# A spectral filter with a gated feed-forward part on one core: a rebuilt prologue, another layout of an intermediate, and stage C moved in the schedule

## The chip, the cores and the metric

The kernel runs on 1 core of one Trainium2 chip. The metric is device time in microseconds (us). "Before" is the kernel before the change, "after" the changed kernel.

## The reference

```python
# x: (8, 3008, 256) float32, filters: (1505, 256)
X = np.fft.rfft(x, axis=1)
y = np.fft.irfft(X * (filt_r + 1j * filt_i), n=3008, axis=1)
t = y.reshape(24064, 256)
gate = np.maximum(t @ w_gate, 0)          # (24064, 1536)
out = (gate * (t @ w_val)) @ w_out        # (24064, 256)
```

## The kernel before

The length 3008 is factored as 94 x 32, so the Fourier part becomes matmuls, done per batch in three stages. Stage A makes the 94-point transform in fp32 and writes it to DRAM (`Abuf`), from where it is read back with other partitions into `at`. Stage B makes the 32-point transform, the product with the filters, and the inverse 32-point transform, and writes the result to DRAM (`Dbuf`), from where it is read into `dC`. Stage C makes the inverse 94-point transform straight into `yT`, the input of the feed-forward part.

The feed-forward part is 47 blocks of 512 tokens, each of 12 steps (`ft`), 564 steps in all. The stages of the next batch are threaded into these steps by hand. Batch 0 is done ahead of them, in a prologue.

```python
def items_a(b):                           # 16 items, one matmul of 512 columns each
    def one(c, j, st):
        psA = ps.tile([128, 512], FP32, tag=fft_tag(), name="psA")
        nc.tensor.matmul(psA[0:NROW], WA[:, :NROW], XF[...][:, o:o + 512], start=True, stop=True)
        nc.scalar.copy(st["asb"][:, j * 512:(j + 1) * 512], psA[0:NROW])
        if j == 3:                        # every fourth item: 384 KB to DRAM
            nc.sync.dma_start(_ap(Abuf[b], ...), st["asb"])
# ...
def load_at(b, c):                        # a quarter of at, after the quarter of Abuf is written
    nc.sync.dma_start(ats[b][32 * c:32 * c + 32], _ap(Abuf[b], ...))
# ... items_b(b): 12 x fwd(g) (psX, then tt and uu), with inv() (psD, then dsb, then Dbuf) two items later
def load_d(b):
    for z in range(NZ):
        dC = sb.tile([NROW, 4, D], BF16, tag="dC", bufs=12)
        nc.sync.dma_start(dC, _ap(Dbuf[b], z * 4 * D, [[N2 * D, NROW], [1, 4 * D]]))
# ... the prologue, from stage B of batch 0 on
for i, f in enumerate(items_b(0, 1)):     # one filler matmul (warm) in each item
    f()
    if i == 4:
        load_vg(2)                        # last third of the value and gate weights
warm(28)                                  # 28 fillers during D's way through DRAM
load_d(0)
hold_gpsimd(dCs[0, 0][0:32, 0, 0:8])      # GpSimd reads dC, so its later loads wait for it
load_o()
load_x(1, nc.gpsimd)
for h in range(2):
    item_c(0, h)
# ... the schedule
LAST = 9
for b in range(1, B):
    end = (b * S // W - 1) * NFT + LAST - 5
    if b == 1:
        s0, sb0 = 13, 33
        every = [sb0 + i + i // 2 for i in range(14)]
    else:
        s0 = end - 54                                     # A starts
        every = [(s0 + 24 | 1) + 2 * i for i in range(14)]  # B starts 25 steps later
    for i, f in enumerate(items_a(b)):
        at_step(s0 + i, f)
    for c in range(4):
        at_step(s0 + 6 + 4 * c, lambda b=b, c=c: load_at(b, c))
    if b + 1 < B:
        at_step(s0 + 17, lambda b=b: load_x(b + 1, nc.gpsimd))
    for i, f in zip(every, items_b(b)):
        at_step(i, f)
    at_step(every[-1] + 1, lambda b=b: load_d(b))
# ... in each step: gate and value matmuls, output matmuls of the last block, the side items, and
if ft in (LAST - 2, LAST + 1) and k + 1 < NB:
    item_c(k + 1, 0 if ft < LAST else 1)
```

In the names of the profile, `psA` is a product of stage A, `psX` and `psD` are the first and the second product of stage B, `psY` is that of stage C, and `psG`, `psV` and `psO` belong to the feed-forward part; `XF` is the input x on the chip. A filler is a matmul whose result (`psJ`) nobody uses; it only keeps TensorE busy.

Of the kernel before, what the change touches and what calls it, by code (L numbers as in the profile page):

```python
# [25 lines left out]


N1, N2 = 94, 32
NROW = 96
NG = 24  # L30
# [9 lines left out]
def _tables():  # L40
    n1 = np.arange(N1)
    n2 = np.arange(N2)
    p = np.arange(16)
    wa = np.zeros((128, NROW + 2))
    for a in range(2):
        wa[np.arange(128) // 16 % 2 == a, NROW + a] = 1.0
    part = 4 * (n1 % 32) + n1 // 32
# [4 lines left out]
    i2t = np.zeros((128, NG, 64))  # L52
    i2u = np.zeros((128, NG, 64))
    for hg in range(48):
        g, a = divmod(hg, 2)
        rows = slice(a * 64, a * 64 + 64)
        f = np.zeros((64, 64))
        t = np.zeros((64, 64))
        u = np.zeros((64, 64))
        k1 = 2 * hg + 2 if hg < 23 else 0 if hg == 23 else 2 * (hg - 24) + 1  # L60
        th = 2 * np.pi * ((n1 * k1) % N1) / N1
        wa[part, 2 * hg] = np.cos(th)
        if k1 not in (0, 47):
            wa[part, 2 * hg + 1] = -np.sin(th)
            m1[2 * hg] = 2.0 * np.cos(th) / S
            m1[2 * hg + 1] = -2.0 * np.sin(th) / S
            k = np.stack([k1 + N1 * p, S - (N1 * (p + 1) - k1)], 1).reshape(32)
            conj = np.tile([1.0, -1.0], 16)
            th = 2 * np.pi * (np.outer(n2, k) % S) / S
            c, s = np.cos(th), np.sin(th)  # L70
            f[:] = np.block([[c, -s], [s, c]])
            ct, st = c.T, s.T
            t[:] = np.block([[ct, st], [-st, ct]])
            u[:] = np.block([[-st, ct], [-ct, -st]]) * np.concatenate([conj, conj])[:, None]
        else:
            m1[2 * hg] = np.cos(th) / S
            th = 2 * np.pi * (np.outer(n2, k1 + N1 * p) % S) / S
            c, s = np.cos(th), np.sin(th)
            f[0:32, 0:32:2] = c
            f[0:32, 32::2] = -s  # L80
            t[0:32:2, 0:32] = 2.0 * c.T
            t[32::2, 0:32] = -2.0 * s.T
            u[0:32:2, 0:32] = -2.0 * s.T
            u[32::2, 0:32] = -2.0 * c.T
            if k1 == 0:
                sign = np.where(n2 % 2 == 0, 1.0, -1.0)
                f[0:32, 32] = sign
                t[0, 0:32] = 1.0
                t[32, 0:32] = sign
                u[0] = 0.0  # L90
                u[32] = 0.0
        f2[lo + 16 * a, g] = f
        i2t[rows, g], i2u[rows, g] = t, u
    tab = np.stack([f2, i2t, i2u], 1).reshape(128, 3, 2, NG // 2, 64).transpose(0, 2, 1, 3, 4)
# [4 lines left out]
def kernel(  # L99
# [31 lines left out]

    Abuf = [dram.tile([NROW * N2, D], BF16, name=f"Abuf{b}") for b in range(B)]
    Dbuf = [dram.tile([NROW * N2, D], BF16, name=f"Dbuf{b}") for b in range(B)]

    WA = consts.tile([128, NROW + 2], FP32)
    XF = [consts.tile([128, NX2 * D], FP32, name=f"XF{c}") for c in range(N2 // NX2)]
# [31 lines left out]
    def place_tables(half):  # L168
        gs = slice(half * H, half * H + H)
        for a in range(2):  # L170
            nc.vector.tensor_scalar(F2[:, gs, a * 64:a * 64 + 64], tabs[:, half, 0],
                                    WA[:, NROW + a:NROW + a + 1], None, op0=ALU.mult)
        for i, t in ((1, I2t), (2, I2u)):
            for a in range(2):
                r = slice(a * 64, a * 64 + 64)
                nc.vector.tensor_copy(t[r, gs, a * 64:a * 64 + 64], tabs[r, half, i])

    def load_filters(half):

        first = 2 - half  # L180
        for fi, (src, dst) in enumerate(FILT):
            for a in range(2):
                r = a * 64
                k1, n = first + 2 * a, H - a
                gs = slice(H * half, H * half + n)
                nc.gpsimd.dma_start(dst[r:r + 31:2, gs, :],
                                    _ap(src, k1 * D, [[N1 * D, 16], [4 * D, n], [1, D]]))
                nc.gpsimd.dma_start(dst[r + 1:r + 32:2, gs, :],
                                    _ap(src, (N1 - k1) * D, [[N1 * D, 16], [-4 * D, n], [1, D]]))
        if half == 0:  # L190
            for fi, (src, dst) in enumerate(FILT):
                nc.gpsimd.dma_start(dst[64:95:2, H - 1::H, :],
                                    _ap(src, 0, [[N1 * D, 16], [47 * D, 2], [1, D]]))
                nyq[fi] = pro.tile([1, D], BF16, tag="nyq", bufs=2, name="nyq")
                nc.gpsimd.dma_start(nyq[fi], _ap(src, (S // 2) * D, [[D, 1], [1, D]]))

    nyq = {}

    def place_filters(half):

        gs = slice(H * half, H * half + H)
        for fi, (src, dst) in enumerate(FILT):
            for a in range(2):
                r = a * 64
                if half == 0:
                    nc.vector.tensor_copy(dst[r + 32:r + 64, gs, :], dst[r:r + 32, gs, :])
                else:
                    nc.sync.dma_start(dst[r + 32:r + 64, gs, :], dst[r:r + 32, gs, :])
            if half == 0:
                nc.vector.tensor_copy(dst[96:97, H - 1, :], nyq[fi])  # L210

    def load_vg(c):
        w = DFF // 3
        for (w_hbm, w_sb) in ((moe_w_val, WvT), (moe_w_gate, WgT)):
            nc.gpsimd.dma_start(w_sb[:, :, c * w:(c + 1) * w],
                                _ap(w_hbm, c * w, [[DFF, 128], [128 * DFF, 2], [1, w]]))

# [6 lines left out]
    def hold_gpsimd(tile_):  # L224

        scr = pro.tile([32, 8], tile_.dtype, tag="scr", bufs=1)
        nc.gpsimd.tensor_copy(scr, tile_)
# [26 lines left out]

    GC = 6
    ats = {}

# [5 lines left out]

    def items_b(b, junk=0):

# [4 lines left out]
        def fwd(g):  # L270
# [6 lines left out]
            nc.vector.tensor_tensor(tt, psX, Ftr[:, g:g + 2, :], op=ALU.mult)  # L277
            if b == 0 and g % 4 == 2:
                xs = pro.tile([128, 2, D], FP32, tag="xs", bufs=2)
# [6 lines left out]
        def inv():  # L286
# [10 lines left out]
            if g + 2 in cuts:  # L297
                nc.sync.dma_start(_ap(Dbuf[b], st["g"] * 128 * D,
                                      [[D, 128], [128 * D, o + 2], [1, D]]), st["dsb"][:, :o + 2, :])

        for g in range(0, NG, 2):
            def both(g=g):
                fwd(g)
                if junk:
                    warm(junk)
                if len(held) > 2:
                    inv()
            yield both
# [4 lines left out]

    def load_d(b):
        for z in range(NZ):
            dC = sb.tile([NROW, 4, D], BF16, tag="dC", bufs=12)
            nc.sync.dma_start(dC, _ap(Dbuf[b], z * 4 * D, [[N2 * D, NROW], [1, 4 * D]]))
            dCs[b, z] = dC
# [83 lines left out]
    load_x(0, nc.sync, 2 * q)  # L402
    for t in (I2t, I2u):
        nc.vector.memset(t, 0.0)
    for (src, dst) in FILT:
        for g in (H - 1, NG - 1):
            nc.vector.memset(dst[64:128, g, :], 0.0)
    load_filters(0)
    load_filters(1)

# [8 lines left out]
    load_at(0, 3)  # L419
    warm(26)  # L420
    place_tables(0)
    place_filters(0)
    place_tables(1)
    place_filters(1)
    hold_gpsimd(ats[0][96:128, NG - 1, 0:8])
    load_vg(0)
    load_vg(1)

    for i, f in enumerate(items_b(0, 1)):
        f()  # L430
        if i == 4:
            load_vg(2)
    warm(28)
    load_d(0)
    hold_gpsimd(dCs[0, 0][0:32, 0, 0:8])
    load_o()
    load_x(1, nc.gpsimd)
    for h in range(2):
        item_c(0, h)
    prologue.close()  # L440
    fs = ctx.enter_context(tc.tile_pool(name="fs", bufs=2))
# [6 lines left out]

    LAST = 9
    for b in range(1, B):  # L450
        end = (b * S // W - 1) * NFT + LAST - 5
        if b == 1:
            s0, sb0 = 13, 33
            every = [sb0 + i + i // 2 for i in range(14)]
        else:
            s0 = end - 54
            every = [(s0 + 24 | 1) + 2 * i for i in range(14)]
        for i, f in enumerate(items_a(b)):
            at_step(s0 + i, f)
        for c in range(4):  # L460
            at_step(s0 + 6 + 4 * c, lambda b=b, c=c: load_at(b, c))
        if b + 1 < B:
            at_step(s0 + 17, lambda b=b: load_x(b + 1, nc.gpsimd))
        for i, f in zip(every, items_b(b)):
            at_step(i, f)
        at_step(every[-1] + 1, lambda b=b: load_d(b))
    prev = None
    for k in range(NB):
        prods = []
        for ft in range(NFT):  # L470
# [3 lines left out]
            for f in side.get(k * NFT + ft, ()):  # L474
                f()
            if ft in (LAST - 2, LAST + 1) and k + 1 < NB:
                item_c(k + 1, 0 if ft < LAST else 1)
        prev = (k, prods)
# [30 lines left out]
```

## Time and profile before

| | before |
|---|---|
| median of the first three runs | 1013.98 us |
| span of the profiled run | 1011.3 us |
| TensorE busy | 956.4 us |
| first feed-forward matmul | 62.2 us |

The page's first part gives busy time, its share of the span and the number of instructions; its fourth part follows the chain of work that ended last, back from the end, and sums it by engine. Two lines of before:

```profile
PE 956.4 (95%) x5934; PEld 567.5 (56%) x6044; DVE 545.6 (54%) x825; ACT 522.2 (52%) x938; POOL 51.5 (5%) x85
...
PE 88%; DMA 5%; ACT 2%; DVE 2%; issue 1%; POOL 1%; SPq 0%; ACTq 0%; POOLq 0%
```

TensorE (PE) is the limit nearly everywhere, so what matters is when it stands still. The view of waits lists for TensorE: which group waited, for whom, us in total, how often, the longest. From it, for before:

```profile
PE psY L338 <- ACT dsb L296: 9.4, 14, 0.7
PE psX L274 <- DMA Fti<-Fti: 7.4, 1, 7.4
PE psX L274 <- DMA at<-Abuf_72: 7.1, 1, 7.1
PE psY L338 <- DMA dC<-Dbuf_80: 5.5, 1, 5.5
PE psD L294 <- POOL uu L281: 3.2, 4, 1.0
```

The reader should see one long list item made of many small waits (`psY` for `dsb`: 9.4 us in 14 waits, wherever a C item falls into a step of B), and three single waits of 5 to 7 us, each for a transfer. Buffers are numbered through the whole program: `Abuf_71` is batch 0 and `Abuf_72` batch 1 in both kernels, but `Dbuf_80` is batch 1 before and batch 0 after.

The table of windows gives, for a stretch in us from the start, its length, the busy time of each engine with its instructions, the granted TensorE clock, the busy share of the DMA engines, and GB/s. Around the wait for `at` of batch 1, before:

```profile
116.00:120.00 4.00, 0.75 (x5) 0.39 (x4) 0.73 (x2) 0.56 (x1) 0.00 (x0) 1.00 0.65 256
120.00:124.00 4.00, 0.11 (x1) 0.11 (x2) 0.00 (x0) 0.00 (x0) 0.00 (x0) 0.60 0.44 115
124.00:128.00 4.00, 4.00 (x20) 2.26 (x20) 2.45 (x4) 0.58 (x1) 0.00 (x0) 0.55 0.00 0
128.00:132.00 4.00, 3.88 (x26) 2.34 (x24) 3.51 (x7) 2.35 (x5) 0.00 (x0) 1.00 0.20 57
```

After some 7 us of idling TensorE runs at about half clock (0.55) for 4 us more, so this wait costs more than its length.

### The profile page before, as it was taken

To read this page: it belongs to the slowest core of one execution; us is meant where nothing else is said; L and a number is where in the kernel's file an instruction comes from. 1 tells how busy PE (TensorE), PEld (TensorE's weight loads), DVE (VectorE), ACT (ScalarE), POOL (GpSimd) and SP (SyncE) were. 2 spreads that over 40 slices of the span, in tenths; PEclk is the share of its full clock that TensorE was granted. 3 is DMA by queue.
4 is the path that set the end of the run, shared out by engine and by line. 5 is a ranking of instruction groups with operands and counts; after the bars stand their busy time and mean duration, and the time that the engine had idled before them with its cause. 6 is when DMAs were issued, how large, how long until landed. Compare 5 with 4: busy or idle time off the path is not lost.

```text
span 1011.3 us, 16206 instructions
## 1 busy us (share of the span) xinstructions
PE 956.4 (95%) x5934; PEld 567.5 (56%) x6044; DVE 545.6 (54%) x825; ACT 522.2 (52%) x938; POOL 51.5 (5%) x85
## 2 busy tenths in 40 slices
PE   8699797999999999999999999999999999999996
PEld 3345364546665556655666456654666556666664
DVE  4443384436754367534865357543675437755551
ACT  3255354555555555555555555555555555555552
POOL 5420000000000100000000000000000000000000
PEclk9899898999999999999999999999999999999998
DMA  9994524154232622436123452415423241231111
GB/s 257 201 266 132 160 53 115 31 175 121 76 110 53 214 74 53 115 92 206 47 71 93 131 172 53 119 38 160 133 77 109 53 115 48 57 112 37 32 32 43
DMA packets 98544, 107.08 MB, mean 106 GB/s; under 512 B 7940, under 2 KB 87236, under 8 KB 96836
## 3 DMA queue, kind: packets, MB, share of 16 engines
q1 hardware_dynamic: 89488, 78.98, 29.0%
q0 software_dynamic: 8576, 25.86, 9.2%
q8 instruction: 47, 0.77, 0.3%
q10 hardware_dynamic: 400, 1.20, 0.3%
q14 instruction: 33, 0.27, 0.1%
HBM read 59.31 MB, written 49.81 MB: 108 GB/s over the span
## 4 chain that ended last, share of the span: by engine, by line
PE 88%; DMA 5%; ACT 2%; DVE 2%; issue 1%; POOL 1%; SPq 0%; ACTq 0%; POOLq 0%
PE psG L354 24%; PE psO L372 23%; PE psV L354 22%; PE psA L243 10%; PE psY L338 2%; PE psX L274 2%; PE psD L294 2%; PE psD L293 2%; DVE prod L359 1%; ACT vsb L357 1%; DMA XF_89<-in_x_dram 1%; ACT dsb L296 1%; DMA Abuf_72<-asb 1%; PE psJ L391 1%; DMA Abuf_71<-asb 1%
## 5 line engine op out<-in xcount | busy, mean ns | idle before, releaser
L359 DVE SCALAR_TENSOR_TENSOR prod<-psG,vsb 128x512 bf16<-128x512 f32 x564 | 389.8, 691 | 397.5 <-ACT vsb L357 381.0
L357 ACT CAST vsb<-psV 128x512 bf16<-128x512 f32 x564 | 331.1, 587 | 223.1 <-PE psV L354 140.6
L372 PE MATMUL psO<-WoT,prod 128*128 128x256 bf16 x2256 | 339.1, 274 | 3.2 <-ACT osb L378 2.5
L354 PE MATMUL psG<-yT,WgT 128*128 128x512 bf16 x1107 | 332.2, 380 | 4.2 <-issue 0.2
L354 PE MATMUL psV<-yT,WvT 128*128 128x512 bf16 x1041 | 318.3, 380 | 1.8 <-ACT yT L343 0.4
L372 PEld LDWEIGHTS <-prod 128*128 128x128 bf16 x2256 | 221.7, 98 | 147.9 <-issue 4.5
L354 PEld LDWEIGHTS <-WgT 128*128 128x128 bf16 x1128 | 110.3, 98 | 135.2 <-issue 2.8
L354 PEld LDWEIGHTS <-WvT 128*128 128x128 bf16 x1128 | 104.5, 98 | 66.4 <-issue 55.5
L246 ACT CAST asb<-psA 96x512 bf16<-96x512 f32 x128 | 74.3, 581 | 120.2 <-PE psA L243 117.0
L296 ACT CAST dsb<-psD 128x512 bf16<-128x512 f32 x96 | 55.9, 586 | 57.0 <-PE psD L294 55.6
L277 DVE TENSOR_TENSOR tt<-psX,Ftr 128x512 bf16<-128x512 f32 x96 | 65.1, 681 | 21.2 <-PE psX L274 21.2
L378 ACT COPY osb<-psO 128x512 f32<-128x512 f32 (+1 forms) x96 | 55.3, 576 | 33.1 <-PE psO L372 27.1
L243 PE MATMUL psA<-XF_89,WA 128*96 128x512 f32 x128 | 65.0, 592 | 1.5 <-DMA XF_89<-in_x_dram 1.5
L243 PE MATMUL psA<-XF_88,WA 128*96 128x512 f32 x128 | 65.1, 592 | 0.4 <-DMA XF_88<-in_x_dram 0.4
L283 DVE TENSOR_TENSOR uu<-psX,Fti 128x512 bf16<-128x512 f32 x90 | 61.2, 680 | 0.0
L274 PE MATMUL psX<-at,F_91 128*128 128x256 bf16 x192 | 37.8, 280 | 15.6 <-DMA Fti<-Fti 7.4
L338 PEld LDWEIGHTS <-dC 96*128 96x128 bf16 x604 | 34.8, 98 | 31.7 <-issue 23.8
L338 PE MATMUL psY<-M_90,dC 96*128 96x94 bf16 (+18 forms) x604 | 37.8, 199 | 14.9 <-ACT dsb L296 9.4
L294 PE MATMUL psD<-uu,I2u 128*128 128x256 bf16 x192 | 47.2, 273 | 3.2 <-POOL uu L281 3.2
L293 PE MATMUL psD<-tt,I2t 128*128 128x256 bf16 x192 | 47.5, 273 | 0.0
L343 ACT CAST yT<-psY 128x512 bf16<-128x512 f32 x47 | 27.5, 585 | 30.8 <-PE psY L338 30.7
L345 DVE CAST yT<-psY 128x512 bf16<-128x512 f32 x47 | 32.1, 684 | 17.3 <-PE psY L338 17.2
(47 smaller groups left out, 202.0 us busy)
## 6 DMA issues: line engine op xcount, KB each, us to landing
XF_88<-in_x_dram POOLq DMA_DIRECT2D x20, 512.0 KB, 7.6
XF_89<-in_x_dram POOLq DMA_DIRECT2D x20, 512.0 KB, 7.7
out_dram<-osb SPq DMA_DIRECT2D x72, 94.0 KB
XF_88<-in_x_dram SPq DMA_DIRECT2D x6, 256.0 KB
XF_89<-in_x_dram SPq DMA_DIRECT2D x3, 512.0 KB
Abuf_71<-asb SPq DMA_DIRECT2D x4, 384.0 KB
at<-Abuf_71 SPq DMA_DIRECT2D x4, 384.0 KB
dC<-Dbuf_79 SPq DMA_DIRECT2D x8, 192.0 KB
```

The lines of the kernel that those rows point to most:

```text
L243: nc.tensor.matmul(psA[0:NROW], WA[:, :NROW], XF[c * NC2 // NX2][:, o:o + 512], start=True, stop=True)
L246: nc.scalar.copy(dst, psA[0:NROW])
L277: nc.vector.tensor_tensor(tt, psX, Ftr[:, g:g + 2, :], op=ALU.mult)
L283: nc.vector.tensor_tensor(uu, psX, Fti[:, g:g + 2, :], op=ALU.mult)
L293: nc.tensor.matmul(psD[:, i], I2t[:, g + i, :], tt[:, i], start=True, stop=False)
L294: nc.tensor.matmul(psD[:, i], I2u[:, g + i, :], uu[:, i], start=False, stop=True)
L296: nc.scalar.copy(st["dsb"][:, o:o + 2, :], psD)
L338: nc.tensor.matmul(psY[:, o:o + w], dCs[b, n2 // 4][:, n2 % 4, h * 128:(h + 1) * 128], M1[:, n1:n1 + w], start=True, stop=True)
L354: nc.tensor.matmul(pt[:, :W], w[:, h, ft * 128:(ft + 1) * 128], yt[:, h, :], start=(h == 0), stop=(h == 1))
L357: nc.scalar.copy(vsb, psV[:, :W])
L359: nc.vector.scalar_tensor_tensor(prod, in0=psG[:, :W], scalar=0.0, in1=vsb, op0=ALU.max, op1=ALU.mult)
L372: nc.tensor.matmul(psO[:, t % 2], prods[ft][:, t * 128:(t + 1) * 128], WoT[:, ft, :], start=(ft == 0), stop=(ft == NFT - 1))
```

## The change

The intent is to start the feed-forward part with more work done: the first stage A items of batch 1 run amid and after stage B of batch 0 in place of filler matmuls. For this x of batch 1 is loaded early, the filters are loaded in longer runs, the tables are placed with a mask, and D is written in runs of 3 KB and read in runs of 512 B. C moves to steps 8 and 10, which B (odd steps) never uses. The diff, cut to its core:

```diff
-            m1[2 * hg] = 2.0 * np.cos(th) / S
-            m1[2 * hg + 1] = -2.0 * np.sin(th) / S
+            m1[48 * a + g] = 2.0 * np.cos(th) / S
+            m1[48 * a + 24 + g] = -2.0 * np.sin(th) / S
 ... (k1 in runs, columns of I2t and I2u in the order of D's new layout)
-                nc.vector.tensor_copy(t[r, gs, a * 64:a * 64 + 64], tabs[r, half, i])
+                nc.vector.tensor_scalar(
+                    t[:, gs, :].rearrange("p g (n a c) -> p g n a c", a=2, c=2)[:, :, :, a, :],
+                    tabs[:, half, i].rearrange("p g (n c) -> p g n c", c=2),
+                    WA[:, NROW + 2 + a:NROW + 3 + a], None, op0=ALU.mult)
 ... (filters: 12 loads of up to 24 KB runs instead of 20; on-chip copies on VectorE and ScalarE)
-                nc.sync.dma_start(_ap(Dbuf[b], st["g"] * 128 * D,
-                                      [[D, 128], [128 * D, o + 2], [1, D]]), st["dsb"][:, :o + 2, :])
+                nc.sync.dma_start(_ap(Dbuf[b], st["g"] * D, [[NG * D, 128], [1, (o + 2) * D]]),
+                                  st["dsb"][:, :o + 2, :])
 ...
+    nc.sync.dma_start(gate, ats[0][96:128, NG - 1, 0:8])   # x of batch 1 behind at of batch 0
+    load_x(1, nc.sync)
+    early = items_a(1)
+    def amid(i):
+        if i < 5:
+            warm(1)
+        else:
+            next(early)()
-    for i, f in enumerate(items_b(0, 1)):
+    for f in items_b(0, amid):
         f()
-        if i == 4:
-            load_vg(2)
-    warm(28)
-    load_d(0)
+    load_vg(DFF // 3, DFF)
+    load_d(0, 0, 2)
     hold_gpsimd(dCs[0, 0][0:32, 0, 0:8])
     load_o()
-    load_x(1, nc.gpsimd)
+    for i in range(5):
+        next(early)()
+        warm(1, 256)
 ...
-    LAST = 9
+    C_AT = (8, 10)
-        end = (b * S // W - 1) * NFT + LAST - 5
-        if b == 1:
-            s0, sb0 = 13, 33
-            every = [sb0 + i + i // 2 for i in range(14)]
-        else:
-            s0 = end - 54
-            every = [(s0 + 24 | 1) + 2 * i for i in range(14)]
+        end = (b * S // W - 1) * NFT + C_AT[0] - 5
+        s0, sb0 = (0, 13) if b == 1 else (end - 54, end - 30 | 1)
 ...
+            at_step(s0 + n - 10 + 4 * c if b > 1 else 4, lambda b=b, c=c: load_at(b, c))
         if b + 1 < B:
-            at_step(s0 + 17, lambda b=b: load_x(b + 1, nc.gpsimd))
+            at_step(s0 + n + 1, lambda b=b: load_x(b + 1, nc.gpsimd))
```

More of the change, by code (lines that the diff above doesn't have):

```diff
@@ L43, in _tables @@
     p = np.arange(16)
-    wa = np.zeros((128, NROW + 2))
+    wa = np.zeros((128, NROW + 4))
     for a in range(2):
+        wa[64 * a:64 * a + 64, NROW + 2 + a] = 1.0
         wa[np.arange(128) // 16 % 2 == a, NROW + a] = 1.0
@@ L53, in _tables @@
     i2u = np.zeros((128, NG, 64))
+    order = np.arange(64).reshape(2, 32).T.reshape(64)
     for hg in range(48):
@@ L59, in _tables @@
         u = np.zeros((64, 64))
-        k1 = 2 * hg + 2 if hg < 23 else 0 if hg == 23 else 2 * (hg - 24) + 1
+        k1 = 1 + g + 24 * a if hg not in (45, 47) else 0 if hg == 45 else 47
         th = 2 * np.pi * ((n1 * k1) % N1) / N1
@@ L75, in _tables @@
         else:
-            m1[2 * hg] = np.cos(th) / S
+            m1[48 * a + g] = np.cos(th) / S
             th = 2 * np.pi * (np.outer(n2, k1 + N1 * p) % S) / S
@@ L92, in _tables @@
         f2[lo + 16 * a, g] = f
-        i2t[rows, g], i2u[rows, g] = t, u
+        i2t[rows, g], i2u[rows, g] = t[:, order], u[:, order]
     tab = np.stack([f2, i2t, i2u], 1).reshape(128, 3, 2, NG // 2, 64).transpose(0, 2, 1, 3, 4)
@@ L132 @@
     Abuf = [dram.tile([NROW * N2, D], BF16, name=f"Abuf{b}") for b in range(B)]
+    gate = dram.tile([32, 8], BF16, name="gate")
     Dbuf = [dram.tile([NROW * N2, D], BF16, name=f"Dbuf{b}") for b in range(B)]
-    WA = consts.tile([128, NROW + 2], FP32)
+    WA = consts.tile([128, NROW + 4], FP32)
     XF = [consts.tile([128, NX2 * D], FP32, name=f"XF{c}") for c in range(N2 // NX2)]
@@ L172, in place_tables @@
                                     WA[:, NROW + a:NROW + a + 1], None, op0=ALU.mult)
-        for i, t in ((1, I2t), (2, I2u)):
-            for a in range(2):
-                r = slice(a * 64, a * 64 + 64)
-                nc.vector.tensor_copy(t[r, gs, a * 64:a * 64 + 64], tabs[r, half, i])
-    def load_filters(half):
-        first = 2 - half
-        for fi, (src, dst) in enumerate(FILT):
-            for a in range(2):
-                r = a * 64
-                k1, n = first + 2 * a, H - a
-                gs = slice(H * half, H * half + n)
-                nc.gpsimd.dma_start(dst[r:r + 31:2, gs, :],
-                                    _ap(src, k1 * D, [[N1 * D, 16], [4 * D, n], [1, D]]))
-                nc.gpsimd.dma_start(dst[r + 1:r + 32:2, gs, :],
-                                    _ap(src, (N1 - k1) * D, [[N1 * D, 16], [-4 * D, n], [1, D]]))
-        if half == 0:
-            for fi, (src, dst) in enumerate(FILT):
-                nc.gpsimd.dma_start(dst[64:95:2, H - 1::H, :],
-                                    _ap(src, 0, [[N1 * D, 16], [47 * D, 2], [1, D]]))
-                nyq[fi] = pro.tile([1, D], BF16, tag="nyq", bufs=2, name="nyq")
-                nc.gpsimd.dma_start(nyq[fi], _ap(src, (S // 2) * D, [[D, 1], [1, D]]))
@@ L197 @@
-    nyq = {}
-    def place_filters(half):
-        gs = slice(H * half, H * half + H)
-        for fi, (src, dst) in enumerate(FILT):
-            for a in range(2):
-                r = a * 64
-                if half == 0:
-                    nc.vector.tensor_copy(dst[r + 32:r + 64, gs, :], dst[r:r + 32, gs, :])
-                else:
-                    nc.sync.dma_start(dst[r + 32:r + 64, gs, :], dst[r:r + 32, gs, :])
-            if half == 0:
-                nc.vector.tensor_copy(dst[96:97, H - 1, :], nyq[fi])
@@ L212, in load_vg, with load_filters @@
-    def load_vg(c):
-        w = DFF // 3
+            for i, t in ((1, I2t), (2, I2u)):
+                nc.vector.tensor_scalar(
+                    t[:, gs, :].rearrange("p g (n a c) -> p g n a c", a=2, c=2)[:, :, :, a, :],
+                    tabs[:, half, i].rearrange("p g (n c) -> p g n c", c=2),
+                    WA[:, NROW + 2 + a:NROW + 3 + a], None, op0=ALU.mult)
+    nyq = []
+    def load_filters():
+        for src, dst in FILT:
+            for a in range(2):
+                r, k1, n = a * 64, 1 + 24 * a, NG - 2 * a
+                nc.gpsimd.dma_start(dst[r:r + 31:2, 0:n, :],
+                                    _ap(src, k1 * D, [[N1 * D, 16], [1, n * D]]))
+                nc.gpsimd.dma_start(dst[r + 1:r + 32:2, 0:n, :],
+                                    _ap(src, (N1 - k1) * D, [[N1 * D, 16], [-D, n], [1, D]]))
+            nc.gpsimd.dma_start(dst[64:95:2, NG - 2:, :],
+                                _ap(src, 0, [[N1 * D, 16], [47 * D, 2], [1, D]]))
+            nyq.append(pro.tile([1, D], BF16, tag="nyq", bufs=2, name="nyq"))
+            nc.gpsimd.dma_start(nyq[-1], _ap(src, (S // 2) * D, [[D, 1], [1, D]]))
@@ L214, in load_vg, with place_filter @@
+    def place_filter(fi, a, half, copy):
+        dst = FILT[fi][1]
+        gs = slice(H * half, H * half + H)
+        r = a * 64
+        copy(dst[r + 32:r + 64, gs, :], dst[r:r + 32, gs, :])
+        if a and half:
+            nc.vector.tensor_copy(dst[96:97, NG - 2, :], nyq[fi])
+    def load_vg(c0, c1):
         for (w_hbm, w_sb) in ((moe_w_val, WvT), (moe_w_gate, WgT)):
-            nc.gpsimd.dma_start(w_sb[:, :, c * w:(c + 1) * w],
-                                _ap(w_hbm, c * w, [[DFF, 128], [128 * DFF, 2], [1, w]]))
+            nc.gpsimd.dma_start(w_sb[:, :, c0:c1],
+                                _ap(w_hbm, c0, [[DFF, 128], [128 * DFF, 2], [1, c1 - c0]]))
@@ L224, in hold_gpsimd @@
     def hold_gpsimd(tile_):
-        scr = pro.tile([32, 8], tile_.dtype, tag="scr", bufs=1)
+        scr = pro.tile(list(tile_.shape), tile_.dtype, tag="scr", bufs=3)
         nc.gpsimd.tensor_copy(scr, tile_)
@@ L255 @@
     GC = 6
+    POOL_G = (2, 4)
     ats = {}
@@ L262, in load_at, with items_b @@
                           _ap(Abuf[b], c * NROW * NC2 * D, [[D, 32], [4 * NC2 * D, NG], [1, D]]))
-    def items_b(b, junk=0):
+    def items_b(b, amid=None):
         held = []
@@ L277, in fwd @@
             nc.vector.tensor_tensor(tt, psX, Ftr[:, g:g + 2, :], op=ALU.mult)
-            if b == 0 and g % 4 == 2:
+            if b == 0 and g % 6 in POOL_G:
                 xs = pro.tile([128, 2, D], FP32, tag="xs", bufs=2)
@@ L303, in both @@
                 fwd(g)
-                if junk:
-                    warm(junk)
+                if amid:
+                    amid(g // 2)
                 if len(held) > 2:
@@ L312, with load_d @@
     dCs = {}
-    def load_d(b):
-        for z in range(NZ):
+    def load_d(b, z0=0, z1=NZ):
+        for z in range(z0, z1):
             dC = sb.tile([NROW, 4, D], BF16, tag="dC", bufs=12)
-            nc.sync.dma_start(dC, _ap(Dbuf[b], z * 4 * D, [[N2 * D, NROW], [1, 4 * D]]))
+            nc.sync.dma_start(dC, _ap(Dbuf[b], z * 4 * NROW * D,
+                                      [[D, NROW], [NROW * D, 4], [1, D]]))
             dCs[b, z] = dC
@@ L402 @@
     load_x(0, nc.sync, 2 * q)
-    for t in (I2t, I2u):
-        nc.vector.memset(t, 0.0)
     for (src, dst) in FILT:
-        for g in (H - 1, NG - 1):
-            nc.vector.memset(dst[64:128, g, :], 0.0)
-    load_filters(0)
-    load_filters(1)
+        nc.vector.memset(dst[64:128, NG - 2:, :], 0.0)
+    hold_gpsimd(XF[0][:, 2 * q - 8:2 * q])
+    load_filters()
     warm(14)
@@ L419 @@
     load_at(0, 3)
-    warm(26)
+    warm(22)
     place_tables(0)
-    place_filters(0)
     place_tables(1)
-    place_filters(1)
-    hold_gpsimd(ats[0][96:128, NG - 1, 0:8])
-    load_vg(0)
-    load_vg(1)
-    for i, f in enumerate(items_b(0, 1)):
-        f()
-        if i == 4:
-            load_vg(2)
-    warm(28)
-    load_d(0)
+    for fi in range(2):
+        for a in range(2):
+            place_filter(fi, a, 0, nc.vector.tensor_copy)
+    for fi in range(2):
+        place_filter(fi, 0, 1, nc.scalar.copy)
+        place_filter(fi, 1, 1, nc.vector.tensor_copy)
+    hold_gpsimd(ats[0][96:128, NG - 1, 0:8])
+    load_vg(0, DFF // 3)
+    nc.sync.dma_start(gate, ats[0][96:128, NG - 1, 0:8])
[7 more added lines that the diff above has]
+    for f in items_b(0, amid):
+        f()
+    load_vg(DFF // 3, DFF)
+    load_d(0, 0, 2)
     hold_gpsimd(dCs[0, 0][0:32, 0, 0:8])
     load_o()
-    load_x(1, nc.gpsimd)
+    for i in range(5):
+        next(early)()
+        warm(1, 256)
     for h in range(2):
         item_c(0, h)
+    load_d(0, 2)
     prologue.close()
@@ L447, in at_step @@
         side.setdefault(s, []).append(f)
-    LAST = 9
+    C_AT = (8, 10)
     for b in range(1, B):
-        end = (b * S // W - 1) * NFT + LAST - 5
-        if b == 1:
-            s0, sb0 = 13, 33
-            every = [sb0 + i + i // 2 for i in range(14)]
-        else:
-            s0 = end - 54
-            every = [(s0 + 24 | 1) + 2 * i for i in range(14)]
-        for i, f in enumerate(items_a(b)):
+        end = (b * S // W - 1) * NFT + C_AT[0] - 5
+        s0, sb0 = (0, 13) if b == 1 else (end - 54, end - 30 | 1)
+        a_items = early if b == 1 else items_a(b)
+        n = 0
+        for i, f in enumerate(a_items):
             at_step(s0 + i, f)
+            n += 1
         for c in range(4):
-            at_step(s0 + 6 + 4 * c, lambda b=b, c=c: load_at(b, c))
+            at_step(s0 + n - 10 + 4 * c if b > 1 else 4, lambda b=b, c=c: load_at(b, c))
         if b + 1 < B:
-            at_step(s0 + 17, lambda b=b: load_x(b + 1, nc.gpsimd))
-        for i, f in zip(every, items_b(b)):
-            at_step(i, f)
-        at_step(every[-1] + 1, lambda b=b: load_d(b))
+            at_step(s0 + n + 1, lambda b=b: load_x(b + 1, nc.gpsimd))
+        for i, f in enumerate(items_b(b)):
+            at_step(sb0 + 2 * i, f)
+        at_step(sb0 + 27, lambda b=b: load_d(b))
     prev = None
@@ L475 @@
                 f()
-            if ft in (LAST - 2, LAST + 1) and k + 1 < NB:
-                item_c(k + 1, 0 if ft < LAST else 1)
+            if ft in C_AT and k + 1 < NB:
+                item_c(k + 1, C_AT.index(ft))
         prev = (k, prods)
```

## The prediction

> **What bounds it now.** TensorE: busy 956 of 1011.3 us, 88% of the chain that ended last. After 62.2 us, where the feed-forward part starts, most 25 us stretches hold 24.8 us of TensorE work (table of windows). Its waits are few and named (waits of TensorE):
> - 7.4 us before stage B of batch 0 (filter copies by DMA);
> - 7.1 us at 117-124 us (B of batch 1 waits for `at`) and 5.5 us at 165-171 us (C waits for `dC` of batch 1);
> - 9.4 us in 14 waits of 0.67 us: `psY` of stage C waits for ScalarE's `dsb` copy, where C sits in a step of B;
> - 3.2 us for GpSimd's `uu` in batch 0.
> After the two long waits the granted clock is 0.55-0.6 for about 4 us. The Trainium skill (TensorE: Matmul & The Clock Gate, Part 1) says idling halves the clock until some 3.4 us of work have passed; the trace agrees. That costs about 2 us each.
>
> **What the change does.**
> 1. A stage A item costs 0.86 us of TensorE. Counted in instruction order, 7 run amid B of batch 0 and 5 after it, so 12 leave the feed-forward part (the title says 11): 10.3 us. They replace 7 fillers and 28 more (0.216 us each) that only kept the array busy.
> 2. Batch 1 gets `at` at step 4 for B at step 13, and its B ends 16 steps before C needs it: the 7.1 and 5.5 us waits and 4 us of slow clock go. But this `at` load meets those of `dC`, the output weights and batch 2's x; I allow 3 us of new waits, here or for the gate weights, two thirds of which are now issued only after B.
> 3. C at steps 8 and 10 never meets B (odd steps): 9.4 us go.
> 4. D is written in 3 KB runs and read in 512 B ones; later batches have 7 steps (9 us) of slack: neutral.
> 5. Prologue: the DMA engines are full from 5 to 39 us. 0.77 MB of on-chip copies go, half of the filter packets become long; filters start after the first x rows. VectorE gets eight masked, strided placements of 128x768, by my estimate up to 0.8 us each (a copy takes 0.36 now), before the filter copies (0.95 us each). I expect B's first product at 36 us instead of 39.9.
> 6. B of batch 0 grows: ScalarE has 12 `dsb`, 8 `xs`, 7 `asb` copies at 0.58 us = 15.7 us; with start, tail and 1-3 us for batch 1's x the loop takes 18 us (15.8 before). Then 5 A items, D's round trip and C: first feed-forward matmul at 59.3 us, only 3 us sooner, but with 10.3 us of A done.
>
> **Sum.** From 62.2 to 1011.3 are 949.1 us. Minus 10.3, 9.4, 7.1, 5.5 and 4, plus 3: 915.8. Starting at 59.3 the span is 975; with 2.7 us between span and measured time, 977 us. About 33 of the 37 us are gained in the feed-forward part, all on TensorE's critical path.
>
> **What would show it.** The `psY` waits on `dsb` gone; no long wait and clock 1.00 between 60 and 175 us; 100 A items instead of 112 after B of batch 0 and its tail; first feed-forward matmul at 57-62 us.
>
> **What would make it wrong.** DMA crowding at 45-85 us (x of two batches, weights, D, A) with a wait of over 5 us before B of batch 1 and a slow clock after it; filters landing late because they start later; new `psX` or `psD` waits where C moved to; B of batch 0 slowed by over 5 us by ScalarE or x.

## More of the kernel before

In order of time on the Sync engine's DMA queue (start, length of the issue, engine, operation), the last write and the last read of A of batch 3 in before:

```profile
345.57 0.33 SPq L261 DMA_DIRECT2D at<-Abuf_74  x1
347.59 0.32 SPq L248 DMA_DIRECT2D Abuf_74<-asb  x1
357.49 0.32 SPq L261 DMA_DIRECT2D at<-Abuf_74  x1
```

The queue issues the last read of `at` only when the last write of `Abuf` has landed, here 9.9 us after the write's issue. The read takes about 4 us more. B then starts with no wait of over 1.1 us in any of batches 2 to 7: this distance has hardly any slack.

## The result, and the profile after

| | before | after |
|---|---|---|
| median | 1013.81 us (4 runs) | 1023.39 us (4 runs, 1022.02 to 1023.95) |
| span of the profiled run | 1011.3 us | 1021.4 us |
| first feed-forward matmul | 62.2 us | 74.8 us |

The ratio is 1.0088, with a 95% interval from 1.0071 to 1.0106. A ratio is the mean time of one kernel's runs over that of the other's of the same rounds, so it is not quite the ratio of the medians quoted. The prediction was 977 us. All outputs are right.

The same two lines of the page, after:

```profile
PE 962.5 (94%) x6010; PEld 568.1 (56%) x6010; DVE 544.8 (53%) x821; ACT 527.9 (52%) x942; POOL 44.0 (4%) x72
...
PE 85%; DMA 13%; ACT 1%; POOL 0%; SPq 0%; issue 0%; DVE 0%; ACTq 0%; POOLq 0%
```

Transfers (DMA) have 13% of the chain that ended last, 5% before. The waits of TensorE, after:

```profile
PE psX L271 <- DMA at<-Abuf_72: 12.3, 1, 12.3
PE psX L271 <- DMA at<-Abuf_71: 7.5, 1, 7.5
PE psY L336 <- DMA dC<-Dbuf_80: 6.5, 1, 6.5
PE psX L271 <- DMA at<-Abuf_74: 5.1, 1, 5.1
PE psX L271 <- DMA at<-Abuf_75: 3.6, 1, 3.6
PE psA L239 <- DMA XF_89<-in_x_dram: 3.5, 1, 3.5
PE psX L271 <- DMA at<-Abuf_77: 3.4, 1, 3.4
...
PE psX L271 <- DMA at<-Abuf_76: 2.4, 1, 2.4
```

The 14 `psY` waits are gone, and so is the wait of batch 1 for its `dC`. In their place stand a wait of 12.3 us for `at` of batch 1 (`Abuf_72`), 6.5 us for `dC` of batch 0 (`Dbuf_80`), and four waits for `at` of batches 3 to 6 (`Abuf_74` to `Abuf_77`), 14.5 us together, at places where before had none over 1.1 us. The 7.5 us for `at` of batch 0 take the place of the filter copies' 7.4.

In the table of windows, four stretches of the prologue, after:

```profile
44.00:46.00 2.00, 0.00 (x0) 0.00 (x0) 0.08 (x1) 0.82 (x2) 2.00 (x2) 0.84 1.02 375
46.00:48.00 2.00, 1.16 (x2) 0.54 (x3) 0.00 (x0) 0.00 (x0) 0.18 (x1) 0.50 1.15 421
48.00:50.00 2.00, 2.00 (x8) 1.06 (x7) 0.00 (x0) 0.86 (x2) 0.00 (x0) 0.50 1.04 384
...
74.00:76.00 2.00, 1.75 (x11) 0.84 (x10) 0.69 (x1) 0.59 (x1) 2.00 (x4) 0.50 0.96 252
```

TensorE meets the first early A item at 43.3 us; x of batch 1 lands at 46.8. After that idling the clock is 0.50, and it is 0.50 again when the feed-forward part starts.

GpSimd's loads of the last weights, and of x of batch 2 (its two halves, `XF_89` and `XF_90`), in order of time, after:

```profile
61.35 0.76 POOL L211 DMA_DIRECT2D WvT<-in_moe_w_val_dram  x1
62.11 0.72 POOL L211 DMA_DIRECT2D WgT<-in_moe_w_gate_dram  x1
...
75.07 1.62 POOL L159 DMA_DIRECT2D XF_89<-in_x_dram  x3
84.53 1.58 POOL L159 DMA_DIRECT2D XF_90<-in_x_dram  x3 [7.84 <-PE psA L239]
```

And on the Sync queue the last writes of D of batch 0, the first two reads of `dC`, the last write of A of batch 1, and the reads of its `at`:

```profile
59.66 3.26 SPq L295 DMA_DIRECT2D Dbuf_80<-dsb  x3
70.35 0.89 SPq L314 DMA_DIRECT2D dC<-Dbuf_80  x2
...
84.87 5.77 SPq L244 DMA_DIRECT2D Abuf_72<-asb  x1
90.75 9.53 SPq L258 DMA_DIRECT2D at<-Abuf_72  x4
```

The last three writes of D were issued by 62.9 us and the reads of `dC` only at 70.35: D's last 128 KB needed 7.7 us in the chain of waits, with 1 MB of weights issued just before. The last write of A of batch 1 took 15.0 us in the same chain, in the middle of the load of x of batch 2. The DMA engines are full from 75 to 103 us (a busy share of 0.93 to 1.23 in every stretch of 3 to 5 us).

The last write and read of A of batch 3, to be laid beside those of before:

```profile
342.98 0.33 SPq L258 DMA_DIRECT2D at<-Abuf_74  x1
344.36 1.64 SPq L244 DMA_DIRECT2D Abuf_74<-asb  x1
356.60 0.32 SPq L258 DMA_DIRECT2D at<-Abuf_74  x1
```

The write now takes 12.2 us instead of 9.9, and B comes one step (1.3 us) sooner after A.

### The profile page after: what moved, and what is told of

The parts are those of the page before. It is cut to its first block, busy times and chain, and to the rows that moved or that the text cites. A ratio compares the mean times of both kernels' runs of the same rounds, so it can differ in the third digit from the quotient of the medians. Undisturbed runs are those within 1.5% of the kernel's fastest.

```text
span 1021.4 us, 16241 instructions
## 1 busy us (share of the span) xinstructions
PE 962.5 (94%) x6010; PEld 568.1 (56%) x6010; DVE 544.8 (53%) x821; ACT 527.9 (52%) x942; POOL 44.0 (4%) x72
## 4 chain that ended last, share of the span: by engine, by line
PE 85%; DMA 13%; ACT 1%; POOL 0%; SPq 0%; issue 0%; DVE 0%; ACTq 0%; POOLq 0%
PE psV L352 22%; PE psG L352 22%; PE psO L370 22%; PE psA L239 10%; PE psY L336 2%; PE psX L271 2%; PE psD L291 2%; PE psD L290 2%; DMA Abuf_72<-asb 1%; DMA XF_89<-in_x_dram 1%; DMA Abuf_74<-asb 1%; DMA Abuf_75<-asb 1%; DMA Abuf_77<-asb 1%; DMA Abuf_76<-asb 1%; DMA XF_90<-in_x_dram 1%; DMA Dbuf_80<-dsb 1%
## 5 line engine op out<-in xcount | busy, mean ns | idle before, releaser
L352 PE MATMUL psV<-yT,WvT 128*128 128x512 bf16 x1128 | 339.9, 383 | 0.5 <-DVE yT L343 0.3
L352 PE MATMUL psG<-yT,WgT 128*128 128x512 bf16 x1128 | 339.0, 382 | 0.0
L271 PE MATMUL psX<-at,F_92 128*128 128x256 bf16 x192 | 38.3, 283 | 34.3 <-DMA at<-Abuf_72 12.3
L239 PE MATMUL psA<-XF_89,WA 128*96 128x512 f32 x128 | 66.9, 607 | 3.5 <-DMA XF_89<-in_x_dram 3.5
L239 PE MATMUL psA<-XF_90,WA 128*96 128x512 f32 x128 | 65.8, 600 | 0.8 <-DMA XF_90<-in_x_dram 0.8
```

Source lines behind the costliest of these rows:

```text
L239: nc.tensor.matmul(psA[0:NROW], WA[:, :NROW], XF[c * NC2 // NX2][:, o:o + 512], start=True, stop=True)
L271: nc.tensor.matmul(psX[:, i], F2[:, g + i, :], at[:, g + i, :], start=True, stop=True)
L352: nc.tensor.matmul(pt[:, :W], w[:, h, ft * 128:(ft + 1) * 128], yt[:, h, :], start=(h == 0), stop=(h == 1))
```

## The experiments

Twelve kernels ran, in four groups; each group ran on one chip and shared its runs of the kernel before. Across groups, ratios are compared, and a difference of ratios is turned into us with 1013 us.

| run | what | median us | ratio to before | 95% interval |
|---|---|---|---|---|
| e1 | before, C in steps 8 and 10 | 999.62 | 0.9865 | 0.9845 to 0.9885 |
| e2 | after, A and B in before's steps | 1002.73 | 0.9895 | 0.9875 to 0.9916 |
| e3 | after, x of batch 2 held | 1005.07 | 0.9925 | 0.9893 to 0.9957 |
| e4 | after, weights earlier | 1017.53 | 1.0044 | 1.0022 to 1.0067 |
| e5 | after, e2 + e3 + e4 | 982.58 | 0.9703 | 0.9685 to 0.9720 |
| e6 | e5, early A from item 8 | 979.35 | 0.9669 | 0.9649 to 0.9689 |
| e7 | e1, A and B in after's steps | 1023.21 | 1.0101 | 1.0083 to 1.0120 |
| e8 | e5, old layout of D | 981.04 | 0.9696 | 0.9666 to 0.9725 |
| e9 | e6, A in after's steps | 979.97 | 0.9677 | 0.9660 to 0.9693 |
| e10 | e6, B in after's steps | 990.88 | 0.9782 | 0.9767 to 0.9797 |
| e11 | e6 in after's steps, every x held | 979.04 | 0.9664 | 0.9643 to 0.9685 |
| e12 | e11, 30 more fillers | 980.33 | 0.9673 | 0.9660 to 0.9686 |

### e1: C off B's steps, alone

```diff
 (kernel before)
-            if ft in (LAST - 2, LAST + 1) and k + 1 < NB:
+            if ft in (LAST - 1, LAST + 1) and k + 1 < NB:
```

> The kernel before with one part of the change alone: stage C's first half in step 8 instead of step 7 of a block (the second stays in step 10), so that C never shares a step with stage B; A and B stay in the steps they had. Theory (C off B's steps is worth its 9.4 us of waits, and the change lost it elsewhere): 14 psY waits on dsb gone, about 1004 us, at waits of later batches stay under 1.5 us. Rival (C in another step only moves the wait to psX, psD or to a later engine): within 3 us of 1014.

The ratio is 0.9865, and 999.62 us is 4 us under what was expected. Its waits of TensorE:

```profile
PE psX L274 <- DMA at<-Abuf: 7.1, 1, 7.1
PE psY L338 <- DMA dC<-Dbuf: 3.7, 1, 3.7
...
PE psY L338 <- ACT dsb L296: 0.7, 1, 0.7
```

Of the 14 waits for `dsb` one is left, and the waits for `at` and `dC` of batch 1 stay. This part of the change is good by itself, and one line brings it.

### e7: the changed kernel's steps, in e1

```diff
 (e1)
-            s0 = end - 54
-            every = [(s0 + 24 | 1) + 2 * i for i in range(14)]
+            s0 = end - 55
+            every = [s0 + 24 + 2 * i for i in range(14)]
```

> e1 (the kernel before with C in steps 8 and 10) with A of batches 2 to 7 one step earlier and B two steps earlier, so 24 steps apart: the steps of the changed kernel. Theory (the steps alone make the waits): at waits of 10 to 16 us over batches 3 to 6 appear with half clock after them, time 1016 to 1021 us. Rival (the waits need the new layout of D or of the tables): at waits under 4 us, time within 3 us of e1's 999.6.

The ratio goes from e1's 0.9865 to 1.0101, some 24 us, a little more than expected. After 140 us its waits of TensorE hold:

```profile
PE psX L274 <- DMA at<-Abuf: 16.3, 5, 4.8
PE psY L338 <- DMA dC<-Dbuf: 4.0, 1, 4.0
```

So the steps alone, with the old prologue, the old layout and the old tables, make a kernel slower than before. The rival, which needs the new layouts, is refuted.

### e2: the same from the other side

```diff
 (kernel after)
-        s0, sb0 = (0, 13) if b == 1 else (end - 54, end - 30 | 1)
+        s0, sb0 = (0, 13) if b == 1 else (end - 53, end - 28 | 1)
```

> The changed kernel with A and B of batches 2 to 7 back in the steps of before (A one step later, B two steps later, so 25 steps apart instead of 24); all else as changed. Theory (the change took one step from a distance that had no slack): the four at waits of batches 3 to 6, 14.5 us together, shrink to under 4 us, and the half clock after them goes: about 1003 to 1006 us. Rival (the transfers of A themselves became slower, by the other layout or memory placement): at waits of over 8 us together remain and the time is above 1015.

After 130 us:

```profile
PE psX L271 <- DMA at<-Abuf: 2.7, 2, 1.8
```

The four waits of 14.5 us have shrunk to two of 2.7 us, and the time falls by 0.0193 of 1013, or 19.6 us. That is more than the waits: the half clock after them goes too. In the table of windows, the clock from 360 to 365 us, just after the wait of batch 3, is 0.50 in after and 1.00 in e2.

### e3: x of batch 2 held back

```diff
 (kernel after)
+        if b == 1:
+            at_step(s0 + n + 1, lambda: nc.gpsimd.tensor_copy(held_at, ats[1][96:128, NG - 1, 0:8]))
         if b + 1 < B:
             at_step(s0 + n + 1, lambda b=b: load_x(b + 1, nc.gpsimd))
```

> The changed kernel, but GpSimd copies 32x8 elements of batch 1's at before it issues the load of batch 2's x, so the load starts only when at has landed. Theory (the 12.3 us wait for at of batch 1 comes from x of batch 2 crowding the write and read of A): the wait falls to under 4 us and the slow clock after it shortens, time about 1011 us. Rival (dC, output weights and A alone fill the DMA engines): the wait stays above 8 us, time within 4 us of 1023.

GpSimd's copy of `at`, and the load behind it:

```profile
93.02 0.18 POOL L471 COPY held_at<-at 32x8 bf16<-32x8 bf16 x1 [20.65 <-DMA at<-Abuf]
93.57 3.19 POOL L160 DMA_DIRECT2D XF<-in_x_dram  x6 [0.37 <-PE psX L272]
```

The load starts at 93.6 us instead of 75.1. Until 110 us the waits for `at` hold those of batches 0 and 1 together:

```profile
PE psX L272 <- DMA at<-Abuf: 8.0, 2, 7.0
```

Batch 1's share is 8.0 minus the 7.0 of batch 0, so 1.0 us instead of 12.3. The time falls by 16.5 us, more than the wait, and more than expected. From 90 to 110 us the clock is 1.00, where after had 0.75, so the half clock goes here too. The size is the least certain of the three: the runs spread from 1002.8 to 1007.4 us, the two intervals together allow some 13 to 20 us, and the trace is of one of the two quicker runs.

### e4: the weights earlier

```diff
 (kernel after)
     def amid(i):
+        if i == 6:
+            load_vg(DFF // 3, DFF)
 ...
-    load_vg(DFF // 3, DFF)
     load_d(0, 0, 2)
```

> The changed kernel, with the last two thirds of the gate and value weights issued at item 6 of stage B of batch 0 instead of after it. Theory (this load crowds the last, 128 KB, write of D, which took 7.7 us, and so makes the 6.5 us wait for dC): write of D under 4 us, wait for dC under 3 us, first feed-forward matmul at 69 to 71 us instead of 74.8, time about 1018 us. Rival (the wait is the round trip of D itself, or the new layout of D is slow): wait for dC stays above 5 us.

The last writes of D and the first reads of `dC` on the Sync queue:

```profile
59.55 3.26 SPq L295 DMA_DIRECT2D Dbuf<-dsb  x3
64.22 0.85 SPq L314 DMA_DIRECT2D dC<-Dbuf  x2
```

Between the end of the last write's issue (62.8) and the first read there are now 1.4 us, where after had 7.4 (62.9 to 70.35); in the chain of waits D's last write takes 1.7 us instead of 7.7. The waits of TensorE until 110 us:

```profile
PE psX L271 <- DMA at<-Abuf: 22.3, 2, 14.6
...
PE psY L336 <- DMA dC<-Dbuf: 0.3, 1, 0.3
```

`dC` is waited for 0.3 us instead of 6.5, and the first feed-forward matmul comes at 68.7 us instead of 74.8. But the wait for `at` of batch 1 grows to 14.6 us: about 2 us of what was gained is given back there. The time falls by 4.5 us.

### e5: the three together

Its edit is the diffs of e2, e3 and e4 in one kernel.

> The changed kernel with the three repairs together: A and B 25 steps apart as in e2, batch 2's x held as in e3, weights earlier as in e4. If the three losses are separate they add: 1023 minus 20.7, 18.3 and 5.9 is 978 to 979 us. If they share one cause (DMA crowding at the start, say), they overlap and the time is above 986 us.

The ratio of 0.9703 is 39.0 us below after's. The three alone gave 19.6, 16.5 and 4.5, together 40.6. Within the intervals the sum cannot be told from that of three separate losses; the expected 978 to 979 us came from subtracting medians and was 4 us too low.

### e6: TensorE meets x later

```diff
 (e5)
-        if i < 5:
+        if i < 8:
             warm(1)
 ...
-    for i in range(5):
+    for i in range(8):
         next(early)()
```

> e5 with the early A items starting at item 8 of stage B of batch 0 instead of item 5 (4 amid B, 8 after it, 12 as before). Theory (B of batch 0 takes 25 us because TensorE meets x of batch 1 before it has landed, idles 3.5 us in order and then runs at half clock until 52 us): the wait for x goes, B ends at 55 to 57 us instead of 61 to 62, first feed-forward matmul at 63 to 65 us instead of about 68.5, time 4 to 5 us under e5. Rival (B is limited by ScalarE's copies, 15.7 us of them, as predicted): B's end moves by under 2 us and e6 is within 2 us of e5.

The first feed-forward matmul is at 64.5 us (e5: 67.7), the clock in the table of windows is 1.00 from 42 us to the end of B, and the time is 3.4 us below e5's by the ratios (4 to 5 were expected). The end of B and D's way through DRAM in the chain of waits (start, length):

```profile
53.69 0.59 ACT dsb L294
...
54.30 6.23 DMA Dbuf<-dsb
...
60.96 2.62 DMA dC<-Dbuf
```

B of batch 0 starts at 36.2 us here and its last copy ends at 54.3 us: 18.1 us, against 25.5 us in after. This is not quite the same loop: it holds 4 early A items instead of 7, and the other 3, about 2.6 us of TensorE (3 x 0.86), now follow it. Of the 7.4 us some 5 are therefore the wait for x and the half clock (an estimate from these numbers). ScalarE's copies are not the limit: 3 of them less are 1.7 us, and against e5 the end of B moved by 7.6 us, from 61.9 to 54.3.

### e8: the old layout of D

```diff
 (e5)
-            m1[48 * a + g] = 2.0 * np.cos(th) / S
+            m1[2 * hg] = 2.0 * np.cos(th) / S
 ... (m1, the order of I2's columns and its placement alike)
-                nc.sync.dma_start(_ap(Dbuf[b], st["g"] * D, [[NG * D, 128], [1, (o + 2) * D]]),
+                nc.sync.dma_start(_ap(Dbuf[b], st["g"] * 128 * D, [[D, 128], [128 * D, o + 2], [1, D]]),
 ...
-            nc.sync.dma_start(dC, _ap(Dbuf[b], z * 4 * NROW * D,
-                                      [[D, NROW], [NROW * D, 4], [1, D]]))
+            nc.sync.dma_start(dC, _ap(Dbuf[b], z * 4 * D, [[N2 * D, NROW], [1, 4 * D]]))
```

> e5 with the old layout of D (written in 512 B runs, read in 2 KB runs; tables and M1 in the order that goes with it). Theory (the layout is neutral once the weights are out of the way): within 3 us of e5; the last write of D to dC's landing in batch 0 within 1.5 us of e5's. Rival (the new layout helps the round trip of D, which is what it is for): the wait for dC of batch 0 is 2 us or more longer here.

The ratio is 0.9696 against e5's 0.9703, and the wait for `dC` of batch 0 is 0.3 against 0.2 us. The layout is neutral here. Both reads and writes stay at 512 B or more, the size from which the Trainium skill (DMA: Bandwidth & Descriptors, Specifications) expects the full rate, and this agrees.

### e9, e10 and e11: what the one step consists of

Two things changed at once for batches 2 to 7, A's step and B's. e9 takes only A's from the changed kernel (26 steps apart), e10 only B's (23 apart), e11 both (24 apart) and holds every x.

```diff
 (e6)
-        s0, sb0 = (0, 13) if b == 1 else (end - 53, end - 28 | 1)
+        s0, sb0 = (0, 13) if b == 1 else (end - 54, end - 28 | 1)      # e9
+        s0, sb0 = (0, 13) if b == 1 else (end - 53, end - 30 | 1)      # e10
+        s0, sb0 = (0, 13) if b == 1 else (end - 54, end - 30 | 1)      # e11, and there:
+        if b + 1 < B:
+            at_step(s0 + n + 3, lambda b=b: nc.gpsimd.tensor_copy(held_at, ats[b][96:128, NG - 1, 0:8]))
+            at_step(s0 + n + 3, lambda b=b: load_x(b + 1, nc.gpsimd))
```

> e6 with A of batches 2 to 7 in the changed kernel's steps (one earlier), B in those of before: 26 steps apart. The last write of A took 9.9 to 12.2 us for batches 3 to 6 in the changed kernel and 7.7 to 10.9 us in e2, where A is a step later. Theory (A's step against the output writes, in step 11 of each block, makes its last write about 2 us slower, more than the step gained): last writes of 10 to 12 us, at waits of 2 to 6 us in all, 982 to 987 us. Rival (only the distance counts): no at waits, 979 us or less.

> e6 with A in the steps of before and B in those of the changed kernel: 23 steps apart. If the write keeps e2's pace of 8 to 11 us, B comes 2.6 us too soon for it: at waits of 8 to 12 us in batches 3 to 6, 991 to 997 us; if the distance alone counts, one step less than the changed kernel's 24 gives waits of over 16 us and over 1000 us.

> e6 with A and B both in the changed kernel's steps, 24 apart, but the load of every next x held on GpSimd until at of the batch has landed (e3's hold for all batches). Theory (the waits come from x's load, which starts by itself the moment its buffer is free and shares the DMA engines with the last write of A): last writes of A fall to under 6 us, no at waits after batch 1, 978 to 981 us although the steps are those of the changed kernel. Rival (the write is slow by itself or by the output writes): waits stay above 8 us and the time above 990 us.

The time from the issue of the last write of A to the issue of the last read, on the Sync queue, in us:

| kernel | A's step | apart | x | batches 3, 4, 5, 6 | mean |
|---|---|---|---|---|---|
| before | late | 25 | free | 9.9, 5.7, 7.6, 8.7 | 8.0 |
| e2 | late | 25 | free | 10.9, 7.7, 9.1, 8.4 | 9.0 |
| e6 | late | 25 | free | 9.8, 6.9, 8.1, 7.0 | 8.0 |
| e10 | late | 23 | free | 10.0, 8.1, 8.3, 5.1 | 7.9 |
| after | early | 24 | free | 12.2, 11.1, 9.9, 10.7 | 11.0 |
| e7 | early | 24 | free | 12.2, 10.3, 11.0, 11.1 | 11.1 |
| e9 | early | 26 | free | 11.6, 9.6, 9.3, 9.7 | 10.1 |
| e11 | early | 24 | held | 7.7, 5.5, 5.6, 5.1 | 6.0 |

For e11, the write and the read of batch 3:

```profile
320.71 1.67 SPq L245 DMA_DIRECT2D Abuf<-asb  x1
328.43 0.32 SPq L259 DMA_DIRECT2D at<-Abuf  x1
```

A's earlier step makes its last write 2 to 3 us slower, and with B two steps and A one step earlier the distance is one step, 1.3 us, shorter (24 against 25); together they are the waits of after. e9 has the slow write, as expected, but its 26 steps cover it: 1.1 us of waits in all, and with 979.97 us it is not in the range of 982 to 987 that was written down for it; its ratio of 0.9677 cannot be told from e6's 0.9669. e10 has the quick write, 8.5 us of waits and 990.88 us, just under the range of 991 to 997. e11 stands in the changed kernel's own steps and has no wait for `at` after batch 1; its writes take 6.0 us on average (batch 3: 7.7) where under 6 was expected. So x's load is worth about 4 of the 10 us that the write takes in the early step; what the other 6 are was not tested. The load issues by itself when the last A item has freed its buffer, whatever step it was emitted in, because nothing else in GpSimd's program holds it back: in after at 84.53 and 344.01 us, 0.3 us before the last writes of A at 84.87 and 344.36. The Trainium skill says of such transfers: "DMAs initiated by the scalar, sync or gpsimd engine will ultimately run on the same 16 DMA engines and interleave with each other" (DMA: Bandwidth & Descriptors, Issuing engines are not separate DMA queues); 10.1 us in e9 against 6.0 in e11 agree.

Why A's step counts for 2 us even with x out of the way (batch 7, which has no x after it: 5.7 us after, 3.5 before; 5.3 in e9, 3.0 in e6) is not shown. The output writes of step 11, on the same queue, come 1 step before the last A item in after and 2 steps before it in before; that is an argument, not a test.

### e12: a warm array before B

```diff
 (e11)
-    warm(22)
+    warm(52)
```

> e11 with 52 filler matmuls instead of 22 before stage B of batch 0, enough to keep TensorE busy until at of batch 0 lands at about 36.5 us (30 more at 0.216 us are 6.5 us). Theory (the half clock from 36.8 to 42 us delays B of batch 0): clock 1.00 from 36 us on, first feed-forward matmul at 62.5 to 63.8 us instead of 64.8, time 977 to 978 us against e11's 979.0. Rival (B is held by the landing of x and by the products' engines, so a warm array only waits sooner): first feed-forward matmul within 0.5 us of 64.8 and the time within 1 us of e11's ratio to the kernel before.

The clock was 1.00 from 30 to 64 us, and nothing came of it: ratio 0.9673 against 0.9664. The first feed-forward matmul came at 66.05 us, later than both expectations had it. Its waits of TensorE:

```profile
PE psY L337 <- DMA dC<-Dbuf: 3.3, 2, 3.0
...
PE psD L292 <- POOL uu L279: 2.7, 3, 1.5
```

TensorE reached the GpSimd products and `dC` sooner, and waited there. So the half clock before B of batch 0 costs nothing that can be measured here; the last write of D took 7.5 us in the chain of waits. The rival was right about the time.

## Why the prediction was wrong, and where it was right

The mechanisms of the gain were right; one term of the sum was missing and three were too small. Predicted was a ratio of 977 to 1014, 0.9635; measured was 1.0088, some 46 us more.

1. **The step that failed most is "C at steps 8 and 10 never meets B (odd steps): 9.4 us go", taken as if C moved alone.** The 9.4 us did go, but the change of C's steps moved A and B of batches 2 to 7 with it through `end`. The only word on these batches, "later batches have 7 steps (9 us) of slack: neutral", looks at D, for which it held; the way from A through DRAM to B had hardly any slack. The sum had 0 for this; e2 measures 19.6 us, and e7 makes a like loss, 24 us, in a kernel that has nothing else of the change but C's steps. It is a slower write (e9, e11) plus a shorter distance (e10).
2. **"I allow 3 us of new waits" was mis-sized.** The crowding was named, with its place, but sized as a small overlap. Removing x of batch 2 from it is worth 16.5 us (e3); the wait was 12.3 us, and half clock followed.
3. **The weights "now issued only after B" had the same 3 us.** They delayed D's last write: 4.5 us in time (e4), 6.1 us at the first feed-forward matmul.
4. **"With start, tail and 1-3 us for batch 1's x the loop takes 18 us".** It took 24.9 us, counted to its last product. That x could slow it by over 5 us was named as a danger, but sized at 1-3. The x came 3.5 us late, and the idling halved the clock, so the first two early A items took 1.7 to 2.0 us each. e6 lets TensorE meet x later and gains 3.4 us. Its loop takes 17.4 us to the last product with 4 A items in it; with all 7 it would be about 20 us (an estimate, adding 3 x 0.86), so the 18 us were some 2 us short even without the wait; no run shows this.

Points 1 to 4 are 19.6 + 16.5 + 4.5 + 3.4 = 44 us, against the 3 allowed. Most of the remaining 5 us is D's way through DRAM: the prediction put the first feed-forward matmul 5.3 us after the end of B, e6 needs 10.2 us from B's last copy, with 6.2 us for D's last write while the DMA engines are full (a busy share of 1.03 from 54 to 60 us, nearly half of it GpSimd's queue, which carries the weights). In e5, where B ends later and the weights are out of the way, the same 128 KB took 1.7 us (a busy share of 0.45 from 62 to 64 us), and the first feed-forward matmul came 5.8 us after B's last copy. So the 5.3 us fit a free DMA, and e6 gives back by crowding part of what its earlier end of B wins. No run changes this alone.

What was right: the `psY` waits were worth their 9.4 us and more (e1: 13.7 us by the ratio, of which 9.4 minus 0.7 are these waits and 1.8 a shorter wait for `dC`; the rest is not assigned). The wait for `dC` of batch 1 went. B of batch 0 began at 37.1 us, predicted 36. The layout of D was neutral (e8). VectorE's strided placements were feared at up to 0.8 us and took 0.42, which hurt nothing. With the four losses repaired, the kernel runs at 979 us, near the 977 predicted for the changed one, and part of that nearness is luck: its feed-forward part starts 5.2 us later than predicted (64.5 against 59.3) and lasts 3.9 us less (911.9 against 915.8, which had 3 us of new waits in it). The value of the early A items (10.3 us in the prediction) was not isolated. From the spans, the part from the first feed-forward matmul to the end is 911.9 us in e6 and 935.7 in e1, so the new prologue with its repairs saves 23.8 us there and gives back 3.0 by starting later.

The best kernels are e6 and e11, at 979.4 and 979.0 us, and the times tell them apart neither from each other nor from e9 and e12. In e6 and e11 the first wait for `at`, 7 us before B of batch 0, is still there.

## What to carry to other kernels

When a change edits a formula that other stages are placed by, list every distance between a producer and its consumer before and after, and read each one's slack from the trace: "no wait" can mean "no slack". A load issued from an otherwise idle engine starts when its buffer is free, not at the step where it was emitted; if it must not crowd a transfer on the critical path, give it something to wait for. When filler work is replaced by real work that needs data, the real work can stall the engine in order, and the stall can bring the half clock back (here 3.5 us of stall, then 0.50).

## What the Trainium skill lacked or had wrong

- DMA: Bandwidth & Descriptors (Issuing engines are not separate DMA queues) says that transfers of different issuers interleave, but gives no size for what this does to a transfer that someone waits for. Here a 384 KB write, from its issue to that of the read behind it, took 10.1 us on average with the next x's load free (e9) and 6.0 us with it held (e11), and 15.0 us at worst (after, batch 1).
- TensorE: Matmul & The Clock Gate (Part 1) names an idle window of about 3.4 us for the fall to half clock. Here a wait of 2.35 us (after, batch 6) was followed by a stretch at 0.50, and one of 1.82 us (e2, batch 3) was not. Ends of matmuls are modelled in these records, so the idle time may be read somewhat short.
